# Turning x from its one copy: half-group moves inside SBUF, planned transfers and a second store queue

## The chip, the cores and the metric

The kernel runs on one core of one Trainium2 chip. What counts is the device time of one execution in microseconds (us), from the first to the last instruction and what lies around them. Five engines run side by side, each with its own queue of instructions that it works off in order: PE (matrix products), ACT (activations), DVE (vector work), POOL and SP (which here only issues transfers, or DMAs). They wait for one another by semaphores.

## The reference

An attention with learned inducing points is followed by a feed-forward layer with squared ReLU. x has 4 batches of 12480 tokens of 128 channels; there are 32 inducing points; the feed-forward layer is 2048 wide.

```python
def mab(q, kv):
    s = scale * (q @ kv.transpose(0, 2, 1))
    s = s - s.max(-1, keepdims=True)
    a = np.exp(s)
    a /= a.sum(-1, keepdims=True) + 1e-09
    return a @ kv
h = mab(I, x)            # 32 points attend to 12480 tokens, in each batch
y = mab(x, h)            # each token attends to the 32 results
...
h = np.maximum(y @ w_in, 0.0)
return (h * h @ w_out).astype(np.float32)
```

## The kernel before

**Tiles.** Tokens go in lanes of 480 (32 x 15). Four lanes make a group of 1920 tokens; a batch has six such groups and one of two lanes, so 26 lanes. A lane is also a block of the feed-forward layer: 104 blocks in all, and they make up most of the time. For the second product of a block, weights and activations are split into a high and a low part of the type fp32r (`hi`, `lo`, `wo_hi`, `wo_lo`), and three products of these stand for one in fp32 (L1027). The first two blocks are "plain": their second product is in fp32 (L984) and needs no split.

**Two attentions.** For each group of a batch, the first attention (class `First`, L396, for batches 1 to 3; `FirstBatch`, L550, for batch 0) needs x twice: as `xn` (rows of tokens, for the mixing product, L518 and L619) and transposed as `xt` (channels on the partitions, for the scores, L465 and L696). In batch 0 PE transposes (L671) and ACT or DVE copies (L254). In later batches `turn_blocks` (L429) loads x a second time: eight transfers for two lanes (L440) bring 32x32 blocks into `xb`, of which there is one buffer, and one DVE instruction turns them into `xt` (L443). `weigh` (L453) then takes scores, a running maximum, the exponential, a transpose of it (`et`) and the mix. In batch 0 the scores of groups 0 to 3 are kept in SBUF until one maximum of all seven groups is known (L569 to L585); then come seven exponentials, transposes and mixes (L603 to L619). `first_end` (L718) joins the sums (`htp`, L740), and multiplies the result by w_in once per batch (`wp`, L753, in four pieces, into `hw`, L757 and L762). `Second` (L780) takes each group's scores against the joined result (`na`, L796), its softmax on DVE and ACT, and copies the weights `sw` four times over the partitions into the tiles `st`, one for each lane (`spread`, L839, four transfers a lane, eight for the lanes of the two-lane groups, L843). A small copy of it (`mini`) serves only the first block of all. A block's first product `h` (L942) reads `hw` and `st`, so the feed-forward layer's first product and the second attention's last are one.

**A block.** `ffn_block` (L916) works in four quads: `h` (L942), relu and square on ACT (L949, L963), the cast `hi` and the rest `lo` on DVE (L968, L973), products into `op` (L1027, one in fp32 from the unsplit weights at L1017). DVE turns the result into `ob` (L1048), and four transfers on SP store it (L1054). The last block of all does that in two parts, of eight and seven rows.

**Who sets the order.** Each step is a task with an engine, a cost in ns, a due time, the tasks it needs and the buffers it takes (`Plan.add`, L68). `Plan.run` (L83) places them at build time: whenever an engine comes free, it takes the task that can start and is due first. So every engine's order is written out before the kernel runs, and an engine that has to wait for one instruction holds up all that stand behind it. The costs and due times are constants in the code. A load of eight blocks of x is booked at 2050 ns (L448), the spread of one lane at 800 (L908), the store of a block at 400 (L1061). x loads are due 20 us ahead of their use (L448). T_MAIN and BLOCK give the due times of the blocks, W_DUE those of the eight pieces of weights, S2_LEAD_0 and S2_LEAD the lead of the second attention, S1_LEAD that of the first. GATES (L193) lists weight tasks that the plan holds back until a step of the mini is done. Buffers are counted in the plan: XBB is the number of `xb`, XTB of `xt` (7, a batch's worth), XNB of `xn` (2), STB of `st` (6).

Of the kernel before, what the change touches and what calls it, by code (L numbers as in the profile page):

```python
# [20 lines left out]
P = 128  # L21
S = 32
# [140 lines left out]
def induced_attention_then_squared_relu_ffn(  # L163
# [232 lines left out]
    class First:  # L396
# [3 lines left out]
        def __init__(self, b, g, due, begun=None):  # L400
# [19 lines left out]
            for h in range(self.L // 2):  # L420
                self.turned.append(self.turn_blocks(h, due - 6000 + 3000 * h))
# [7 lines left out]
        def turn_blocks(self, h, due):  # L429
            b = self.b  # L430
            bb = Buffer("xb")
            v = {}

            def load():
                v["xb"] = xb_pool.tile([P, 2, NR, S], F32, tag="xb", name=f"xb_{self.n}_{h}")
                for l in range(2):
                    at = self.at + (2 * h + l) * LANE
                    rows = x[b, at:at + LANE, :].rearrange("(t r) (g c) -> g t r c", r=NR, c=S)
                    for c in range(P // S):
                        nc.sync.dma_start(v["xb"][c * S:(c + 1) * S, l], rows[c])  # L440

            def turn():
                nc.vector.transpose(  # L443
                    self.xt_tile()[:, 2 * h:2 * h + 2].rearrange("c l r t -> c (l r t)"),
                    v["xb"].rearrange("p l r c -> p (l r c)"),
                )
# [103 lines left out]
    class FirstBatch:  # L550


        def __init__(self, due, step, mix_due, mix_step):
            self.s = s = state.setdefault(0, {"xt": {}, "bxt": {}, "turned": {}})
            s["first"] = self
            self.sp, self.xn, self.bsp = {}, {}, {}
            self.loaded, self.tops, bxs = [], [], []
            v = {}
# [3 lines left out]
            kept = NG - 3  # L562

            for g in range(NG):
                self.group(g, due + step * g, g < kept, bare)

            def lanes():
                v["mx"] = tiny.tile([P, 1], F32, tag="mx", name="mx_0")
                nc.vector.tensor_reduce(v["mx"], bare[:, 0, :NG], axis=AX.X, op=ALU.max)  # L569

            def lanes2():
                v["lanes"] = tiny.tile([P, Q], F32, tag="lanes", name="lanes_0")
                nc.vector.tensor_scalar_mul(v["lanes"], lane_q, v["mx"])

            def gather():
                v["tops"] = self.last_sp[:, LANE:LANE + Q]
                nc.tensor.matmul(v["tops"], same, v["lanes"], start=True, stop=True)

            def most():
                v["top"] = tiny.tile([P, 1], F32, tag="top", name="top_0")  # L580
                nc.vector.tensor_reduce(v["top"], v["tops"], axis=AX.X, op=ALU.max)

            def shift():
                self.neg = tiny.tile([P, 1], F32, tag="neg", name="neg_0", bufs=4)
                nc.vector.tensor_scalar_mul(self.neg, v["top"], -scale)  # L585

            d = mix_due
            bg = self.bsp[NG - 1]
            t = add("DVE", 100, lanes, d - 3000, self.tops)
            t = add("DVE", 110, lanes2, d - 3000, [t])  # L590
            t = add("PE", 110, gather, d - 3000, [t], reads=[bg])
            t = add("DVE", 100, most, d - 3000, [t], reads=[bg])
            shifted = add("DVE", 70, shift, d - 3000, [t])
            bn = Buffer("s")
            powered, mixed = None, None
            for g in range(NG):
# [4 lines left out]
                def power(g=g, R=R, c=c):  # L601
# [3 lines left out]
                        bias=self.neg[:R], scale=scale, accum_out=bare[:R, 1, g:g + 1],  # L605
# [8 lines left out]
                def mix(g=g, R=R, c=c):  # L614
                    if g == 0:
                        v["nb"] = early_bank("nb_0")[:, :C]
                    for r in range(NR):
# [3 lines left out]
                            start=g == 0 and r < Q, stop=g == NG - 1 and r >= NR - Q,  # L621
                        )

                d = mix_due + mix_step * g
                powered = add("ACT", 820, power, d, [shifted, powered], takes=[be], reads=[self.bsp[g]])
                t = add("DVE", wide_ns(LANE), turn_e, d + 1000, [powered], takes=[bet], reads=[be])
                mixed = add("PE", 950, mix, d + 2000, [t, mixed], mode="n", takes=[] if g else [bn],
                            reads=[bet, self.bx[g]] + ([bn] if g else []))

            def add_h():  # L630
                self.acc = att.tile([P, C], F32, tag="hacc", name="hacc_0")
# [11 lines left out]
        def group(self, g, due, kept, bare):  # L643
# [4 lines left out]
            if g == 0:  # L648
                self.bxs = {}
# [493 lines left out]
```

## Time and profile before

| what | value |
|---|---|
| median of 3 | 1652.6 us (1652.34 to 1657.75) |
| the profiled execution | 1653.15 us |
| its span, first to last instruction | 1651.4 us |
| instructions | 22141 |
| bytes moved | 101.30 MB in 389085 packets, 368848 of them under 512 B |
| read from HBM, written to it | 48.94 MB, 25.56 MB |
| transfers `xb<-in_x_dram` | 312 of 60 KB, median 2.6 us from issue to landing |
| transfers `st<-sw` of 60 KB | 380, median 2.0 us |
| transfers `out_dram<-ob` of 60 KB | 412, median 2.2 us |

Times in the profile are microseconds from the span's start, unless marked ns. PEld is the loading of weights into PE, beside its products. "SPq" is SP's queue, which issues transfers. A row such as `PE h L942 <- DMA st<-sw` says that PE stood idle ahead of an instruction of line 942 that writes `h`, and that the landing of the transfer that fills `st` from `sw` ended the wait. In the chain of work that ended last, each piece stands with its start, its length and its name; it is followed back from the last instruction, at each step to what released it.

### The profile page before, as it was taken

The numbers are of one execution on the slowest core, as the hardware profiler recorded it, in microseconds if no ns is written. First come the engines' busy times: TensorE is split into PE (matmuls) and PEld (weight loads), VectorE is DVE, ScalarE is ACT, GpSimd is POOL, SyncE is SP. The second block draws the span as 40 slices with busy tenths as digits, with TensorE's granted clock in tenths as the row PEclk, the third lists the DMA queues.
The fourth block names the chain that finished last, engine by engine and source line by source line (L and its number), as shares of the span: only waits on it lengthen the run. The fifth ranks groups of instructions, "written<-read, shape, count | busy, mean of one in ns | idle before, by whom it ended". The sixth has DMA issues, their size and how long they took to land.

```text
span 1651.4 us, 22141 instructions
## 1 busy us (share of the span) xinstructions
PE 1615.4 (98%) x8004; PEld 1282.1 (78%) x8004; DVE 1535.6 (93%) x1457; ACT 1526.3 (92%) x1425; POOL 45.1 (3%) x39
## 2 busy tenths in 40 slices
PE   7889999999999999999999999999999999999998
PEld 5368787887778788888877778878787878888886
DVE  6759999999989999999999999999999999999997
ACT  5679999999989999999989999999999999999997
POOL 0000000000000000000000000000000000000000
PEclk9999999999999999999999999999999999999999
DMA  7441533422243333323233334233012212111211
GB/s 246 111 87 43 100 56 69 70 44 60 49 86 71 59 68 79 57 49 77 41 63 78 76 60 91 47 67 73 13 31 43 40 24 51 37 31 19 43 30 19
DMA packets 389085, 101.30 MB, mean 61 GB/s; under 512 B 368848, under 2 KB 385136, under 8 KB 388976
## 3 DMA queue, kind: packets, MB, share of 16 engines
q1 hardware_dynamic: 388976, 99.89, 29.8%
q8 instruction: 63, 1.03, 0.3%
q14 instruction: 46, 0.38, 0.1%
HBM read 48.94 MB, written 25.56 MB: 45 GB/s over the span
## 4 chain that ended last, share of the span: by engine, by line
PE 89%; DVE 5%; SPq 2%; issue 2%; DMA 1%; ACT 1%; DVEq 0%; POOL 0%; ACTq 0%
PE op L1027 57%; PE h L942 21%; PE op L1017 5%; DVE lo L973 2%; SPq L440 1%; PE nb L518 1%; PE na L796 1%; DVE hi L968 1%; PE sp L465 1%; PE op L984 1%; PE xtp L671 1%; SPq L843 1%; PE wp L753 1%; DVE hw L762 0%; DMA st<-sw 0%
## 5 line engine op out<-in xcount | busy, mean ns | idle before, releaser
L949 ACT ACTIVATE g<-h 128x960 f32<-128x960 f32 x832 | 780.4, 983 | 63.8 <-PE h L942 46.5
L973 DVE TENSOR_TENSOR lo<-g,hi 128x1920 fp32r<-128x1920 f32 (+1 forms) x409 | 823.7, 2015 | 15.2 <-DVE z L823 0.3
L963 ACT ACTIVATE g<-g 128x1920 f32<-128x1920 f32 (+1 forms) x419 | 760.2, 1814 | 4.5
L942 PE MATMUL h<-st,hw 128*128 128x480 f32 x1664 | 516.0, 392 | 6.4 <-DMA st<-sw 5.1
L968 DVE CAST hi<-g 128x1920 fp32r<-128x1920 f32 (+1 forms) x409 | 442.6, 1082 | 47.7 <-ACT g L963 39.7
L1027 PE MATMUL op<-hi,wo_hi 128*128 128x480 f32 x1530 | 442.5, 403 | 0.0
L1027 PE MATMUL op<-hi,wo_lo 128*128 128x480 f32 x1530 | 435.7, 383 | 0.0
L1027 PE MATMUL op<-lo,wo_hi 128*128 128x480 f32 x1530 | 415.4, 381 | 0.6 <-DVE lo L973 0.6
L942 PEld LDWEIGHTS h<-st,hw 128*128 128x128 f32 x1664 | 309.0, 188 | 93.9 <-issue 28.2
L1027 PEld LDWEIGHTS op<-hi,wo_hi 128*128 128x128 f32 x1530 | 286.2, 188 | 81.4 <-issue 36.6
L1027 PEld LDWEIGHTS op<-lo,wo_hi 128*128 128x128 f32 x1530 | 286.6, 188 | 54.8 <-issue 5.9
L1027 PEld LDWEIGHTS op<-hi,wo_lo 128*128 128x128 f32 x1530 | 287.2, 188 | 49.1 <-issue 3.0
L1017 PE MATMUL op<-g,wo_whole 128*128 128x480 f32 x204 | 98.9, 566 | 0.0
L820 POOL TENSOR_SCALAR z<-z 128x15 f32<-128x15 f32 (+1 forms) x28 | 44.0, 1571 | 1535.8 <-DVE z L816 1453.3
L1048 DVE STREAM_TRANSPOSE ob<-op 128x480 f32<-128x480 f32 (+1 forms) x105 | 70.3, 670 | 3.2 <-PE op L1027 2.9
L443 DVE STREAM_TRANSPOSE xt<-xb 128x960 f32<-128x960 f32 x39 | 45.2, 1159 | 14.3 <-DMA xb<-in_x_dram 11.3
L1017 PEld LDWEIGHTS op<-g,wo_whole 128*128 128x128 f32 x204 | 38.3, 189 | 7.5 <-issue 1.6
L518 PE MATMUL nb<-xn,et 128*32 128x128 f32 (+1 forms) x630 | 23.4, 282 | 5.7 <-DVE et L510 5.7
L518 PEld LDWEIGHTS nb<-xn,et 128*32 128x32 f32 (+1 forms) x630 | 17.5, 112 | 13.0 <-DVE et L510 6.5
L796 PE MATMUL na<-xt,hT 128*32 128x480 f32 (+1 forms) x224 | 26.9, 551 | 0.0
L465 PE MATMUL sp<-xt,indT 128*32 128x480 f32 x156 | 22.5, 578 | 2.2 <-DVE xt L443 2.2
L254 ACT CAST sw<-a 128x480 fp32r<-128x480 f32 (+1 forms) x25 | 14.2, 570 | 8.9 <-DVE a L830 8.8
(132 smaller groups left out, 469.7 us busy)
## 6 DMA issues: line engine op xcount, KB each, us to landing
out_dram<-ob SPq DMA_DIRECT2D x412, 60.0 KB, 2.2
xn<-in_x_dram SPq DMA_DIRECT2D x24, 960.0 KB, 5.1
st<-sw SPq DMA_DIRECT2D x380, 60.0 KB, 2.0
xb<-in_x_dram SPq DMA_DIRECT2D x312, 60.0 KB, 2.6
xn<-in_x_dram SPq DMA_DIRECT2D x4, 480.0 KB, 5.1
hi_i<-in_moe_w_in_dram SPq DMA_DIRECT2D x2, 512.0 KB, 14.5
lo_i<-in_moe_w_in_dram SPq DMA_DIRECT2D x2, 512.0 KB, 17.4
hi_o<-in_moe_w_out_dram SPq DMA_DIRECT2D x2, 512.0 KB, 4.3
```

The lines of the kernel that those rows point to most:

```text
L443: nc.vector.transpose(self.xt_tile()[:, 2 * h:2 * h + 2].rearrange("c l r t -> c (l r t)"), v["xb"].rearrange("p l r c -> p (l r c)"),)
L518: nc.tensor.matmul(v["nb"][c * M:(c + 1) * M, :], self.et[:R, r, :], self.xn[:R, r, :], start=r < Q, stop=r >= NR - Q,)
L796: nc.tensor.matmul(v["na"][i * M:(i + 1) * M, :W], s["hT"][:, :M], cols[:, c:c + W], start=True, stop=True,)
L820: E.tensor_scalar(v["z"], v["z"], 1e-9, 0.0, ALU.add, ALU.add)
L942: nc.tensor.matmul(c["hp"][:, l, :LANE], s["hw"][:, f * P:(f + 1) * P], second.st[k], start=True, stop=True,)
L949: nc.scalar.activation(v["g"][:, 2 * i:2 * i + 2, :], c["hp"][:, :, :LANE], AF.Relu)
L963: nc.scalar.activation(v["g"][:, h], v["g"][:, h], AF.Square)
L968: nc.vector.tensor_copy(v["hi"][:, h], v["g"][:, h])
L973: nc.vector.tensor_sub(v["lo"][:, h], v["g"][:, h], v["hi"][:, h])
L1017: nc.tensor.matmul(w["op"][:, :LANE], wo_whole, v["g"][:, 3, :], start=False, stop=False)
L1027: nc.tensor.matmul(w["op"][:, :LANE], pools["wo"][wo][:, 4 * j + l, :], v[name][:, l, :], start=(j == x_ == 0 and l == 0), stop=(j == NQ - ...
L1048: nc.vector.transpose(w["ob"][:, rows].rearrange("p r c -> p (r c)"), w["op"][:, rows.start * S:rows.stop * S])
```

## The change

It has five parts.

1. In batches 1 to 3, x is no longer loaded a second time. Each group is turned in two halves, of 64 channels each, straight from `xn` into one of two buffers `xb` (XBB is 2), by one DVE instruction; then transfers inside SBUF move each block of 32 channels of each lane to its place in `xt`: eight for half a group of four lanes, four for half a group of two. So the transfers' number (16 or 8 a group) stays, and the groups of two lanes need two turns where they needed one. The turn waits for `xn`; the move waits for the turn and takes the `xt` buffer.
2. Transfers are booked in the plan with other costs: 1240 ns for each lane of a move, 2480 for each piece of a spread, 2600 for a store. Moves have the due time of their turn.
3. Batch 0's first attention runs in two parts, groups 0 to 4 and groups 5 and 6, each with a maximum of its own; the first part's sums are faded when they are added to the second's. Five groups' scores are kept, not four, and an exponential waits for its own group's kept scores.
4. The last block's second store goes out by ACT's queue, not SP's.
5. Constants: due times, leads and steps have other values; the pieces 1 to 3 of batch 0's `wp` go into the banks `m`, not `h`, and they and the first copy of `hw` are held back by other steps of the mini; the mini's `sk` takes a buffer of `xb`.

```diff
-    GB, HB, LB, OB, MB, STB, XTB, XNB, XBB = 3, 2, 2, 2, 2, 6, 7, 2, 1
-    T_MAIN, BLOCK = 42100.0, 15100.0
+    GB, HB, LB, OB, MB, STB, XTB, XNB, XBB = 3, 2, 2, 2, 2, 6, 7, 2, 2
+    T_MAIN, BLOCK = 48600.0, 15100.0
-    W_DUE = [11900.0, 21100.0, 24900.0, 30200.0, 41500.0, 46000.0, 50000.0, 53300.0]
-    FIRST_DUE, FIRST_STEP, MIX_DUE, MIX_STEP, MINI_DUE = 6000.0, 2600.0, 25000.0, -1000.0, -800.0
-    S2_LEAD, S2_LEAD_0, S2_STEP, S1_LEAD, S1_STEP = 44500.0, 26000.0, 1600.0, 11100.0, 3000.0
+    W_DUE = [20500.0, 27300.0, 31000.0, 32500.0, 43500.0, 42700.0, 47000.0, 53600.0]
+    FIRST_DUE, FIRST_STEP, MIX_DUE, MIX_STEP, MINI_DUE = 5800.0, 3100.0, 22400.0, 200.0, -1000.0
+    S2_LEAD, S2_LEAD_0, S2_STEP, S1_LEAD, S1_STEP = 40500.0, 30000.0, 1400.0, 10900.0, 3600.0
...
-        s0=m.ready[0], s1=m.ready[0], s2=m.ready[0], s3=m.ready[0], w0_1=m.normed, w0_2=m.normed, w0_3=m.normed,
+        s0=m.ready[0], s1=m.ready[0], s2=m.ready[0], s3=m.ready[0], w0_1=m.ready[0], w0_2=m.ready[0], w0_3=m.ready[0], p0_0=m.powered,
...
-    SPLIT_DUE, SPLIT_STEP, PLAIN_DUE = 64000.0, 0.0, 9500.0
+    KEPT = 5
+    SPLIT_DUE, SPLIT_STEP, PLAIN_DUE = 65000.0, 200.0, 6000.0
-    G1_DUE, SQ_DUE, HI_DUE, LO_DUE, OP_DUE = -1500.0, 6000.0, 2500.0, 6500.0, 10300.0
-    OT_DUE = 7900.0
+    G1_DUE, SQ_DUE, HI_DUE, LO_DUE, OP_DUE = -2500.0, 6200.0, 4500.0, 6500.0, 14100.0
+    OT_DUE = 6100.0
...
-            for h in range(self.L // 2):
-                self.turned.append(self.turn_blocks(h, due - 6000 + 3000 * h))
+            for h in range(2):
+                self.turned.append(self.turn_blocks(h, due - 8000 + 4000 * h))
             self.weigh(due + 2000, S1_STEP)
...
         def turn_blocks(self, h, due):
-            def load():
-                v["xb"] = xb_pool.tile([P, 2, NR, S], F32, tag="xb", name=f"xb_{self.n}_{h}")
-                for l in range(2):
-                    at = self.at + (2 * h + l) * LANE
-                    rows = x[b, at:at + LANE, :].rearrange("(t r) (g c) -> g t r c", r=NR, c=S)
-                    for c in range(P // S):
-                        nc.sync.dma_start(v["xb"][c * S:(c + 1) * S, l], rows[c])
-
             def turn():
+                v["xb"] = xb_pool.tile([P, 2, NR, S], F32, tag="xb", name=f"xb_{self.n}_{h}")
                 nc.vector.transpose(
-                    self.xt_tile()[:, 2 * h:2 * h + 2].rearrange("c l r t -> c (l r t)"),
-                    v["xb"].rearrange("p l r c -> p (l r c)"),
+                    v["xb"][:R].rearrange("p j r t -> p r j t"),
+                    self.xn[:R, :, 2 * h * S:2 * (h + 1) * S].rearrange("p r (j c) -> p r j c", j=2),
                 )
-            t = state["blocks"] = add("SP", 2050, load, due - 20000, [state.get("blocks"), self.begun], takes=[bb], late=0)
-            t = state["turn"] = add("DVE", 1090, turn, due, [t, state.get("turn"), self.begun],
-                                    takes=[] if h else [self.bt], reads=[bb] + ([self.bt] if h else []))
-            return t
+            def move():
+                xt = self.xt_tile()
+                for j in range(2):
+                    c0 = (2 * h + j) * S
+                    for q in range(self.L):
+                        nc.sync.dma_start(xt[c0:c0 + S, q], v["xb"][q * M:(q + 1) * M, j])
+
+            t = state["turn"] = add("DVE", 1090, turn, due, [self.loaded, state.get("turn"), self.begun],
+                                    takes=[bb], reads=[self.bx])
+            return add("SP", 1240 * self.L, move, due, [t] + self.turned, late=0, takes=[] if h else [self.bt],
+                       reads=[bb] + ([self.bt] if h else []))
...
+            self.kept = kept = KEPT
+            for i, span in enumerate([range(kept), range(kept, NG)]):
+                prev = self.part(i, span, prev, bare, [mix_due - kept * mix_step, mix_due][i], mix_step)
...
+            def fade():
+                v["fade"] = tiny.tile([P, 1], F32, tag="fade", name="fade_0")
+                nc.scalar.activation(v["fade"], prev["neg"], AF.Exp, bias=new["neg"], scale=-1.0)
...
+                    nc.vector.scalar_tensor_tensor(new["acc"], prev["acc"], v["fade"], v["nb"], ALU.mult, ALU.add)
...
-            if b:
+            if b or k:
                 v["wp", k] = bank(f"wp_{b}_{k}")
...
-                t = self.ready[k] = state["spread"] = add("SP", 800, lambda k=k: spread(k), d + 8 * step,
+                t = self.ready[k] = state["spread"] = add("SP", 2480 * len(to[k]), lambda k=k: spread(k), d + 8 * step,
...
         def store(rows):
+            queue = nc.scalar if last_block and rows.start else nc.sync
             for c in range(P // S):
-                nc.sync.dma_start(out_v[c][:, rows], w["ob"][c * S:(c + 1) * S, rows])
+                queue.dma_start(out_v[c][:, rows], w["ob"][c * S:(c + 1) * S, rows])
...
-            add("SP", 400, lambda rows=rows: store(rows), end + 6000, [t])
+            add("ACT" if last_block and rows.start else "SP", 2600, lambda rows=rows: store(rows), end + 6000, [t])
```

More of the change, by code (lines that the diff above doesn't have):

```diff
@@ L561, in __init__, with part, most_of @@
             nc.gpsimd.memset(bare[:, 1], 0.0)
-            kept = NG - 3
+            self.kept = kept = KEPT
             for g in range(NG):
-                self.group(g, due + step * g, g < kept, bare)
+                self.group(g, due + step * g, bare)
+            prev = None
+            for i, span in enumerate([range(kept), range(kept, NG)]):
+                prev = self.part(i, span, prev, bare, [mix_due - kept * mix_step, mix_due][i], mix_step)
+        def part(self, i, span, prev, bare, due, step):
+            v, new = {}, {}
+            last = span[-1]
+            def most_of():
+                v["mx"] = tiny.tile([P, 1], F32, tag="mx", name=f"mx_0_{i}")
+                nc.vector.tensor_reduce(v["mx"], bare[:, 0, span.start:span.stop], axis=AX.X, op=ALU.max)
@@ L567, in lanes @@
             def lanes():
[L568 to L572, printed above, removed]
+                v["lanes"] = tiny.tile([P, Q], F32, tag="lanes", name=f"lanes_0_{i}")
                 nc.vector.tensor_scalar_mul(v["lanes"], lane_q, v["mx"])
             def gather():
-                v["tops"] = self.last_sp[:, LANE:LANE + Q]
+                v["tops"] = self.bank[last][:, LANE:LANE + Q]
@@ L587, in __init__ @@
[L587 to L593, printed above, removed]
+                new["neg"] = tiny.tile([P, 1], F32, tag="neg", name=f"neg_0_{i}", bufs=4)
+                if prev:
+                    nc.vector.scalar_tensor_tensor(new["neg"], v["top"], -scale, prev["neg"], ALU.mult, ALU.min)
+                else:
+                    nc.vector.tensor_scalar_mul(new["neg"], v["top"], -scale)
@@ new lines, in fade @@
+            def fade():
+                v["fade"] = tiny.tile([P, 1], F32, tag="fade", name="fade_0")
+                nc.scalar.activation(v["fade"], prev["neg"], AF.Exp, bias=new["neg"], scale=-1.0)
+            bg = self.bs[last]
+            t = add("DVE", 100, most_of, due - 3000, [self.tops[g] for g in span])
+            t = add("DVE", 110, lanes, due - 3000, [t])
+            t = add("PE", 110, gather, due - 3000, [t], reads=[bg])
+            t = add("DVE", 100, most, due - 3000, [t], reads=[bg])
@@ L594, in __init__ @@
+            shifted = new["shifted"] = add("DVE", 70, shift, due - 3000, [t, prev and prev["shifted"]])
             bn = Buffer("s")
-            powered, mixed = None, None
-            for g in range(NG):
+            powered, mixed = prev and prev["powered"], prev and prev["mixed"]
+            for g in span:
                 R = M * lanes_of[g]
@@ L620, in mix @@
                             v["nb"][k * M:(k + 1) * M, :], c["et"][:R, r, :], self.xn[g][:R, r, :],
-                            start=g == 0 and r < Q, stop=g == NG - 1 and r >= NR - Q,
+                            start=g == span[0] and r < Q, stop=g == last and r >= NR - Q,
                         )
-                d = mix_due + mix_step * g
-                powered = add("ACT", 820, power, d, [shifted, powered], takes=[be], reads=[self.bsp[g]])
+                d = due + step * (g - span[0])
@@ L630, in add_h @@
+            new["powered"], new["mixed"] = powered, mixed
             def add_h():
[L631 to L639 removed]
@@ L641, in induced_attention_then_squared_relu_ffn @@
-        bx = property(lambda self: self.bxs)
-        def group(self, g, due, kept, bare):
+                new["acc"] = att.tile([P, C], F32, tag="hacc", name=f"hacc_0_{i}")
+                if prev:
+                    nc.vector.scalar_tensor_tensor(new["acc"], prev["acc"], v["fade"], v["nb"], ALU.mult, ALU.add)
+                else:
+                    copy(new["summed"], new["acc"], v["nb"])
+                self.acc = new["acc"]
+            def add_z():
+                new["z"] = tiny.tile([P, 1], F32, tag="z", name=f"z_0_{i}")
+                nc.vector.tensor_reduce(new["z"], bare[:, 1, span.start:span.stop], axis=AX.X, op=ALU.add)
+                self.sum = new["z"]
+                if prev:
+                    self.sum = tiny.tile([P, 1], F32, tag="zs", name="zs_0")
+                    nc.vector.scalar_tensor_tensor(self.sum, prev["z"], v["fade"], new["z"], ALU.mult, ALU.add)
@@ L644, in group @@
+            f = add("ACT", 250, fade, due, [shifted]) if prev else None
+            d = due + step * len(span)
+            self.totalled = new["totalled"] = add("DVE", 250 if prev else 100, add_z, d, [powered, f, prev and prev["totalled"]])
+            self.summed = new["summed"] = add("DVE", 260, add_h, d + 1000, [mixed, f, prev and prev["summed"]], reads=[bn])
+            return new
+        def group(self, g, due, bare):
             s = self.s
@@ L708, in group @@
             t = add("PE", 950, score, due + 1200, turned_, mode="n", takes=[bs], reads=[bt])
[L709 to L710 removed]
+            self.tops[g] = add("DVE", wide_ns(LANE), top, due + 2000, [t], reads=[bs])
+            if g < self.kept:
                 self.bsp[g] = Buffer("st")
```

55 lines of the change are left out of this document (23 added, 32 removed).

## The prediction

> **What bounds the kernel now.** I read the page's busy times first, then a table by stage, then who waited for whom, then the chain of work that ended last and the transfer queue in the stages that the table marks.
>
> ```profile
> PE 1615.4 (98%) x8004; PEld 1282.1 (78%) x8004; DVE 1535.6 (93%) x1457; ACT 1526.3 (92%) x1425; POOL 45.1 (3%) x39
> ```
>
> PE is busy almost throughout, so the average tells little: what a change can win lies where PE stands still. The table by stage shows where that is (us of the stage, then busy us of PE, weight loads, DVE, ACT, POOL, the granted clock, the share of the DMA engines, GB/s).
>
> ```profile
> core 0 of [0], span 1651.4 us
> core 0: us, PE busy (x) PEld busy (x) DVE busy (x) ACT busy (x) POOL busy (x), PEclk, DMA share, GB/s
> 20.00:45.00 25.00, 18.26 (x283) 12.62 (x281) 23.05 (x51) 14.31 (x28) 0.00 (x0) 0.86 0.60 191
> 45.00:54.00 9.00, 7.50 (x29) 2.67 (x29) 6.43 (x19) 2.97 (x6) 0.00 (x0) 0.81 0.68 165
> 54.00:72.00 18.00, 14.39 (x49) 6.19 (x50) 14.82 (x27) 16.18 (x18) 1.01 (x1) 1.00 0.23 41
> 72.00:90.00 18.00, 12.25 (x59) 7.08 (x56) 9.39 (x20) 9.01 (x11) 0.29 (x1) 0.81 0.38 68
> 90.00:108.00 18.00, 18.00 (x56) 10.19 (x55) 6.52 (x7) 15.68 (x14) 0.00 (x0) 1.00 0.62 136
> 420.00:470.00 50.00, 47.23 (x237) 34.85 (x236) 45.26 (x51) 42.45 (x43) 0.32 (x1) 0.99 0.29 60
> 470.00:830.00 360.00, 360.00 (x1785) 290.51 (x1785) 347.66 (x319) 343.51 (x317) 12.00 (x7) 1.00 0.33 64
> 830.00:880.00 50.00, 47.65 (x266) 35.30 (x265) 46.80 (x53) 41.69 (x43) 0.32 (x1) 1.00 0.35 72
> 1630.00:1651.40 21.40, 14.85 (x65) 11.81 (x63) 13.37 (x13) 9.75 (x9) 0.00 (x0) 0.96 0.16 23
> ```
>
> From 470 to 830 PE never rests, and neither removed loads nor a quieter HBM can shorten that stretch. There are four places left: the start, where DVE is the full engine (23.05 of 25 us); the first blocks, 54 to 90 us, where PE lacks 9.4 us (3.61 and 5.75); the two changes of batch, where it lacks 2.8 and 2.4; and the end. PE's waits after the start name the causes (waiter, releaser: us in total, times, longest).
>
> ```profile
> PE nb L518 <- DVE et L510: 5.7, 1, 5.7
> PE h L942 <- DMA st<-sw: 5.1, 2, 2.8
> PE sp L465 <- DVE xt L443: 2.2, 1, 2.2
> ```
>
> The first and third lie in the first blocks; there the transfer queue and the chain read:
>
> ```profile
> 63.03 5.24 SPq L440 DMA_DIRECT2D xb<-in_x_dram  x8
> 68.38 7.54 SPq L843 DMA_DIRECT2D st<-sw  x12
> 76.02 6.23 SPq L440 DMA_DIRECT2D xb<-in_x_dram  x8
> ```
>
> ```profile
> 81.62 2.79 DMA xb<-in_x_dram
> ...
> 84.72 1.18 DVE xt L443
> 85.90 0.53 DVE z L816
> 86.44 0.60 DVE et L510
> 87.08 1.93 PE nb L518 x30
> ```
>
> SP needs about 0.65 us for each of these issues, so eight are 5.2 to 6.2 us, where the plan booked 2050 ns, and four spreads are 2.5 us, where it booked 800. DVE stood behind a load that the plan believed landed, and PE behind DVE. The second wait, for st, is at the changes of batch:
>
> ```profile
> 458.19 5.27 SPq L440 DMA_DIRECT2D xb<-in_x_dram  x8
> 463.56 2.48 SPq L843 DMA_DIRECT2D st<-sw  x4
> ```
>
> ```profile
> 465.46 1.95 DMA st<-sw
> ```
>
> Eight loads for a group that is scored tens of us later (they go by a due time 20 us ahead of their use) stand in front of the four copies that the next block cannot start without.
>
> **The start (L553 and on).** Now all seven groups of batch 0 share one maximum; after the change groups 0 to 4 have their own, and 5 and 6 follow with a fade. The chain shows:
>
> ```profile
> 23.25 0.94 PE sp L696 x8
> ...
> 31.72 0.14 DVE neg L585
> ...
> 44.24 0.47 PE htp L740 x2
> ```
>
> ```profile
> 53.97 0.48 PE L942 MATMUL h<-st,hw 128*128 128x480 f32 x1
> ```
>
> The last row, of PE's timeline, is the first h of the first block. By my count of the score rows, the one at 23.25 is the fifth group. From the shift at 31.72 to the join at 44.24 are 12.5 us for seven groups, 1.8 each, with weight decoding between them on DVE. If only two groups were left behind the last maximum, that would be 3.6 us, a gain of 8.9 at the most. Against it stands DVE at 23.05 of 25 us: the decoding only changes places (W_DUE), and what is put off is due again soon after. Added are a second chain of maximum, shift and sums, some seven tiny instructions at the 0.14 us of the shift's row, 1.0 us, and one more copy of scores (KEPT is 5, not 4), perhaps half a microsecond. Bounds: 8.9 gained to 1.5 lost. I take half of the gain less the additions: **4 gained**. The moved banks and gates of the first products (wide, GATES) work in the same chain and are in that figure; the mini's sk now takes an xb buffer, which is free before the first turn, so it costs nothing unless that turn is early.
>
> **The first blocks.** Per full group, 16 loads of x go and 16 moves inside SBUF come: the number of issues on SP is the same, and by the rows above their price is too (5.24/8 = 0.65 for a load, 7.54/12 = 0.63 for a copy of the moves' shape). So SP is not relieved. What changes is what DVE waits for: its turn now reads xn, which one big load brought, and no longer a burst of eight issues. The 5.7 us wait cannot come in this form. And the plan now books 4960 ns for eight moves, 2480 for four spreads, 2600 for a store. But a move is a new wait in SP's queue: it waits for the turn, for its half-group buffer and for an xt buffer that the last batch's scores must release; behind it on SP stand spreads, for which PE's h waits, and stores, for whose ob buffers DVE's L1048 and then the op bank wait. The moves' due times are ahead of those of the first twelve spreads, so a burst may still stand in front of them. At stake are the 9.4 us of idle PE, and the clock: 72 to 90 shows 0.81 on 12.25 busy us, at most 2.3 lost. Bounds: 11.7 gained to 0. I leave two waits of the size of the 2.2 us row, 4.4 in all: **7 gained**. The Trainium skill (TensorE: Matmul & The Clock Gate, Part 1) says that an idle PE falls to half its clock and needs some 3.4 us of work to get it back. The row 0.81 agrees that the gate closed here; by that rule the sum would be a microsecond or so better if the long wait goes, since its wake goes too.
>
> **The changes of batch.** No load of a far group can slip in front of st any more, since a move needs a turned half-group and a free xt buffer; and the second attention starts from an earlier due time (S2_LEAD_0 30 us, not 26). Bounds: the 5.1 us that PE waited for st, to 0 if moves of the next batch's first group take the loads' place: they are due 18.9 and 14.9 us ahead of the block (10.9 + 8, and 4 later), the spread 18.8 (30 less 8 steps of 1.4). I take **4 gained**.
>
> **The end.** The last eight stores:
>
> ```profile
> 1645.37 3.80 SPq L1054 DMA_DIRECT2D out_dram<-ob  x8
> DMA to landing us min/median/max: 1.6/1.6/1.7
> ```
>
> 3.80/8 is 0.475 us an issue. With the second four on ACT they no longer stand behind the first four: 1.9 us saved if ACT issues as fast, which no row shows; 0 if it is twice as slow. I take **1.7 gained**. The Trainium skill (DMA: Bandwidth & Descriptors, Issuing engines are not separate DMA queues) speaks against this edit: both queues feed the same engines, and only issue time is saved, "which is usually small relative to the DMA itself". By that the term would be near 0 and the sum 1.7 us worse. Here 1.9 us of issue stand beside 1.6 to land, so it isn't small.
>
> **The steady stretch.** DVE turns 42 half-groups in place of 39 (the groups of two lanes now need two). A half-group is still 960 elements a partition, but read and written in runs of 32.
>
> ```profile
> L443 DVE STREAM_TRANSPOSE xt<-xb x39: 1117/1167/1205, 61.8 to 1191.1; 128x960 f32<-128x960 f32 x39
> L254 DVE COPY xt<-xtp x3: 1090/1092/1225, 9.5 to 21.3; 128x896 f32<-128x896 f32 x2, 128x1024 f32<-128x1024 f32 x1
> ```
>
> The second row writes xt in runs of 32 and takes 1.22 ns an element, the first 1.22 without them; so runs seem to cost nothing. The three more turns are 3.5 us of DVE; from 470 to 830 it has 12.3 of 360 to spare. Bounds 0 to 3.5 lost, **1 lost** taken. Cover gone, each turn's delay would be PE's.
>
> **The sum.** -4 - 7 - 4 - 1.7 + 1 = -15.7. The profiled execution took 1653.15 us around its span of 1651.4; the median is 1652.6, 0.55 below it. Predicted: 1652.6 - 15.7 = 1636.9, so 1637. About 0.5% (8.3 us) is what a measurement of this kernel tells from no change.
>
> **Rivals.** *More is won*: two groups only behind the last maximum, all of the waits gone: -8.9 - 11.7 - 5.1 - 1.9 = -27.6, 1625. For it: those waits come from wrong bookings, which are mended. Against: DVE's full start. Chance 0.13.
>
> *The queue keeps its bursts*: as many issues at the same price, moves ahead of spreads as the loads were. Only start, end and the three turns count: -4 - 1.7 + 1 = -4.7, 1648. For it: equal issue counts and the due times above. Against: the bookings now match the rows. Chance 0.16.
>
> *Slower, the score waits for the moves*: until now x was prefetched to the turn, and PE waited for a turn once in 21 groups. Now behind each turn come 8 issues and 2 us to land before PE may score, and SP, in order, often sits at the head of its queue:
>
> ```profile
> SPq L1054 <- DVE ob L1048: 398.5, 54, 25.9
> ```
>
> A move that stands behind such a store is late, and PE, in order too, stands at the score with all blocks' products behind it. Priced by the longest wait for st, 2.8 us: at all 21 groups 58.8, at 11 of them 30.8 - 15.7 = +15, 1668. It outweighs the gain from 6 groups on (15.7/2.8), and makes it slower by over 0.5% from 9. Against it: moves are due 10 and 6 us ahead of the score, and PE's order comes from a plan that now books them fully. Chance 0.11.
>
> **How the numbers follow.** Forecast 0.60, own range 1627 to 1642 (the start and the first blocks both at their best, or both at half). With 0.13 at 1625 and 0.16 at 1648 around it, 1620 to 1656 leaves out the third rival and some tails, 0.2. Faster 0.60 + 0.13 = 0.73, same 0.16, slower 0.11.
>
> **What would show it.** Right: the first h near 50; no wait of DVE's turn for a transfer; PE idle in the first 36 us of blocks below 5 us; no wait of h for st at the changes of batch; two queues at the end, with the last landing 1.7 us after less issuing. Wrong: PE waits at sp for moves, a median turn above 1.3 us, or gaps in the stretch that is full now.

## The result and the profile after

| | before | after |
|---|---|---|
| median of 4 runs each | 1653.25 us (1652.34 to 1657.75) | 1643.59 us (1642.27 to 1643.93) |
| ratio after/before, 95% interval | | 0.9935 (0.9915 to 0.9954) |
| the profiled execution's span | 1651.4 us | 1641.5 us |

By the medians the kernel became 9.7 us faster, 0.58%; by the ratio, 0.65%, and its interval leaves no change out. That is 6 us short of the 15.7 us that the sum gave: 1643.59 us lies inside the wide range of 1620 to 1656, but 1.6 us above the forecast's own range, 1627 to 1642. The page of the kernel after has these lines of busy times, packets, bytes from HBM, the turn (busy us, mean ns of one, then the idle time of DVE ahead of it) and the moves (median us to landing):

```profile
PE 1615.2 (98%) x8006; PEld 1277.3 (78%) x8006; DVE 1538.8 (94%) x1476; ACT 1525.8 (93%) x1418; POOL 48.8 (3%) x39
...
DMA packets 249308, 101.29 MB, mean 62 GB/s; under 512 B 219088, under 2 KB 245360, under 8 KB 249200
...
HBM read 29.77 MB, written 25.56 MB: 34 GB/s over the span
...
L437 DVE STREAM_TRANSPOSE xb<-xn 128x960 f32<-128x960 f32 (+1 forms) x42 | 48.9, 1164 | 15.0 <-DMA out_dram<-ob 6.3
...
xt<-xb SPq DMA_DIRECT2D x312, 60.0 KB, 2.0
```

The change does what it says: 19 MB less are read from HBM, packets fall by a third, there are 42 turns of 1164 ns and as many moves as there were loads. The column to look at is the last of the turn's row: DVE stood idle for 15.0 us ahead of turns, for transfers. The table by stage of the kernel after (columns as in the prediction: PE, weight loads, DVE, ACT, POOL, granted clock, DMA share, GB/s):

```profile
20.00:45.00 25.00, 20.41 (x301) 11.44 (x300) 23.04 (x63) 14.26 (x29) 0.00 (x0) 0.93 0.43 132
45.00:54.00 9.00, 5.33 (x12) 3.37 (x13) 8.53 (x21) 4.15 (x6) 0.00 (x0) 0.66 0.70 275
54.00:72.00 18.00, 17.23 (x58) 7.49 (x56) 16.99 (x29) 15.52 (x19) 0.89 (x1) 0.98 0.31 73
72.00:90.00 18.00, 17.90 (x82) 9.98 (x81) 6.51 (x15) 16.68 (x17) 0.29 (x1) 1.00 0.41 88
90.00:108.00 18.00, 14.48 (x61) 9.68 (x59) 9.27 (x7) 16.27 (x14) 0.00 (x0) 1.00 0.50 127
420.00:470.00 50.00, 50.00 (x278) 37.45 (x277) 47.83 (x53) 46.17 (x47) 0.32 (x1) 1.00 0.42 100
470.00:830.00 360.00, 359.38 (x1786) 289.00 (x1785) 347.83 (x324) 342.90 (x315) 11.99 (x7) 1.00 0.29 62
830.00:880.00 50.00, 49.91 (x250) 37.10 (x249) 48.42 (x50) 45.04 (x44) 1.23 (x2) 1.00 0.37 85
```

From 54 to 90 us PE's idle time fell from 9.4 to 0.9 us, and the clock of 72 to 90 from 0.81 is full. At the two changes of batch it fell from 5.1 to 0.1. But from 90 to 108, where PE was full, it now lacks 3.5 us. PE's waits from 54 us to the end of the kernel after (waiter, releaser: us in total, times, longest) name that one, and no wait for `st` or at `sp` is left:

```profile
PE op L1049 <- DVE hi L990: 4.4, 2, 3.8
PE h L964 <- ACT g L971: 0.7, 2, 0.4
```

It is one chain over three engines. SP's queue, then DVE's and PE's timeline of the kernel after (start, length, what; in brackets the idle time ahead and its releaser):

```profile
84.03 10.60 SPq L863 DMA_DIRECT2D st<-sw  x16
94.67 5.02 SPq L447 DMA_DIRECT2D xt<-xb  x8
99.74 0.58 SPq L412 DMA_DIRECT2D xn<-in_x_dram  x1
```

```profile
97.54 2.16 DVE L995 TENSOR_TENSOR lo<-g,hi 128x1920 fp32r<-128x1920 f32 x1
105.96 1.18 DVE L437 STREAM_TRANSPOSE xb<-xn 128x960 f32<-128x960 f32 x1 [6.26 <-DMA out_dram<-ob]
107.06 1.12 DVE L990 CAST hi<-g 128x1920 fp32r<-128x1920 f32 x1
```

```profile
103.35 1.13 PE L964 MATMUL h<-st,hw 128*128 128x480 f32 x4
108.24 1.15 PE L1049 MATMUL op<-hi,wo_hi 128*128 128x480 f32 x4 [3.76 <-DVE hi L990]
```

Sixteen spreads and eight moves occupied SP for 15.6 us; only then was the big load of the next group's `xn` issued, although its buffer had been free since about 78 us (the mix that last read it ran from 77.1 to 78.0). The load takes some 5 us to land. The turn reads `xn`, so it waited 6.3 us. The row's releaser is a store, but the turn doesn't touch what a store reads; e6 below shows that it was the load. Behind the turn, in order, stood the cast `hi`, and behind that PE's products. The wait has an aftermath in the clock. The same table for the 12 us around it:

```profile
104.00:108.00 4.00, 0.48 (x3) 0.08 (x1) 2.04 (x2) 3.33 (x3) 0.00 (x0) 1.00 0.47 91
108.00:112.00 4.00, 3.76 (x14) 2.59 (x18) 4.00 (x4) 0.60 (x1) 0.00 (x0) 0.67 0.00 0
112.00:116.00 4.00, 4.00 (x20) 2.19 (x13) 4.00 (x7) 3.52 (x4) 0.00 (x0) 0.91 0.19 47
```

A clock of 0.67 and then 0.91 over 4 us each loses 1.3 + 0.4 = 1.7 us more, so the wait of 3.76 us cost about 5.5. The Trainium skill (TensorE: Matmul & The Clock Gate, Part 1) has the clock fall to half after an idle window of some 3.4 us, and come back after as long a busy one; the trace agrees, since 1.7 us lost at half speed are 3.4 us of it.

### The profile page after: what moved, and what is told of

Its sections match the earlier page's. It is cut to its first block, busy times and chain, and to the rows that moved or that the text cites. A ratio compares the mean times of both kernels' runs of the same rounds, so it can differ in the third digit from the quotient of the medians.

```text
span 1641.5 us, 22177 instructions
## 1 busy us (share of the span) xinstructions
PE 1615.2 (98%) x8006; PEld 1277.3 (78%) x8006; DVE 1538.8 (94%) x1476; ACT 1525.8 (93%) x1418; POOL 48.8 (3%) x39
## 4 chain that ended last, share of the span: by engine, by line
PE 92%; DVE 3%; SPq 2%; ACT 1%; DMA 1%; issue 1%; DVEq 0%; ACTq 0%
PE op L1049 60%; PE h L964 22%; PE op L1039 5%; PE na L816 1%; PE nb L519 1%; PE sp L466 1%; DVE lo L995 1%; SPq L863 1%; PE wp L773 1%; SPq L447 1%; ACT g L971 0%; PE op L1006 0%; DVE hi L990 0%; PE xtp L691 0%; DMA xn<-in_x_dram 0%
## 5 line engine op out<-in xcount | busy, mean ns | idle before, releaser
L964 PE MATMUL h<-st,hw 128*128 128x480 f32 x1664 | 529.1, 400 | 2.4 <-DVE st L898 1.5
L1049 PE MATMUL op<-hi,wo_hi 128*128 128x480 f32 x1530 | 434.5, 394 | 4.4 <-DVE hi L990 4.4
L1049 PE MATMUL op<-hi,wo_lo 128*128 128x480 f32 x1530 | 428.8, 381 | 0.0
L1049 PE MATMUL op<-lo,wo_hi 128*128 128x480 f32 x1530 | 424.3, 382 | 0.6 <-DVE lo L995 0.4
L840 POOL TENSOR_SCALAR z<-z 128x15 f32<-128x15 f32 (+1 forms) x28 | 47.7, 1703 | 1522.2 <-DVE z L836 1509.2
L437 DVE STREAM_TRANSPOSE xb<-xn 128x960 f32<-128x960 f32 (+1 forms) x42 | 48.9, 1164 | 15.0 <-DMA out_dram<-ob 6.3
L832 ACT ACTIVATE d<-d 128x480 f32<-128x480 f32 (+1 forms) x28 | 16.2, 579 | 5.9 <-DVE d L829 5.8
```

Source lines behind the costliest of these rows:

```text
L437: nc.vector.transpose(v["xb"][:R].rearrange("p j r t -> p r j t"), self.xn[:R, :, 2 * h * S:2 * (h + 1) * S].rearrange("p r (j c) -> p r j ...
L840: E.tensor_scalar(v["z"], v["z"], 1e-9, 0.0, ALU.add, ALU.add)
L964: nc.tensor.matmul(c["hp"][:, l, :LANE], s["hw"][:, f * P:(f + 1) * P], second.st[k], start=True, stop=True,)
L1049: nc.tensor.matmul(w["op"][:, :LANE], pools["wo"][wo][:, 4 * j + l, :], v[name][:, l, :], start=(j == x_ == 0 and l == 0), stop=(j == NQ - ...
```

## The experiments

My theory after the result: the gain came from the bookings alone (part 2 of the change), since the plan now knows how long SP is held; and x from its one copy (part 1) costs time, since DVE's turn, and what stands behind it in order, hangs on SP's queue twice, for a late `xn` and for a free `xb`. The rival is the one that the change's looks suggest: it gained by reading 19 MB less, and the bookings only rearranged the waits. The start and the end were tested for their own terms. Each run has its own median of the kernel before, on the same chip, beside it; gains are best compared by the ratios.

**e1, the end alone.** The kernel before, with the last store's second part on ACT's queue.

```diff
+            queue = nc.scalar if last_block and rows.start else nc.sync
             for c in range(P // S):
-                nc.sync.dma_start(out_v[c][:, rows], w["ob"][c * S:(c + 1) * S, rows])
+                queue.dma_start(out_v[c][:, rows], w["ob"][c * S:(c + 1) * S, rows])
```

> The kernel before with one edit: the second of the last two stores goes out by ACT's queue. If issue time on SP was what the end waited for (theory A), the last landing comes about 1.6 us earlier and the time is 1651.6 against 1653.2. If both queues share what limits the end, nothing changes: 1653.2.

1652.78 us against 1654.02 (ten and nineteen runs), ratio 0.9987 (0.9978 to 0.9997): 1.2 us by the medians, 2.1 by the ratio. In its profile 5.05 us pass from the end of the last product to the end of the span, where it was 6.55 before. In the kernel after, the two queues' last issues are these:

```profile
1637.35 1.95 ACTq L1077 DMA_DIRECT2D out_dram<-ob  x4
```

```profile
1637.05 1.86 SPq L1077 DMA_DIRECT2D out_dram<-ob  x4
```

ACT issues at 0.49 us apiece, SP at 0.47: side by side they need 2.3 us where the prediction's row showed 3.8.

**e2, the start in one part.** The kernel after, with one maximum for all seven groups.

```diff
-            for i, span in enumerate([range(kept), range(kept, NG)]):
+            for i, span in enumerate([range(NG)]):
```

> The changed kernel with batch 0's first attention in one part again (one maximum for all seven groups), all else as changed. Theory A (the start is full of DVE work that only changes places): within 1.5 us of the changed kernel, 1642 to 1645. Theory C (the two parts are worth the 4 us that were forecast): 1647 to 1648, with the first h later and what PE loses up to 90 us greater by 4.

1645.31 against 1654.02, ratio 0.9941 (0.9925 to 0.9956). The first h stands at 57.7 us, 8.4 later than in the kernel after (49.3), and the time is 1.7 us longer by the medians, 1.0 by the ratios, whose intervals overlap: just above theory A's range by the medians, and short of theory C's. The due times here were set for two parts; the kernel before, with its own, has its first h at 53.97. So against this run a first block that starts 8.4 us earlier brings 1 to 2 us at the end. The chain of the kernel after shows part of the reason:

```profile
39.63 0.47 PE htp L760 x2
...
43.55 4.25 DMA lo_o<-in_moe_w_out_dram
...
48.46 0.51 ACT st L894
...
49.30 1.97 PE h L964 x4
```

The join is 4.6 us earlier than before, as is the first h (49.30, not 53.97). But from 45 to 54 us DVE is busy for 8.53 of 9 us and PE for only 5.33, at a clock of 0.66: the decoding that was put off is due there. The last product of block 0 ends at 65.0 us, where it ended at 66.7 before, and block 1's first `op` starts at 67.1, not 67.5: little of the 4.7 us is left. And e2 has no wait at 104 us (PE is busy for all 18 us from 90 to 108), so it is no clean price of the two parts: the kernel after has the earlier start and that wait. e6 below has two parts without the wait, and stands 4.3 us below e2 by the ratios, with intervals that just overlap.

**e3, the same bytes from HBM.** The kernel after, but each move is replaced, at its place in the queue, by a transfer of 60 KB from HBM.

```diff
-                        nc.sync.dma_start(xt[c0:c0 + S, q], v["xb"][q * M:(q + 1) * M, j])
+                        at = self.at + q * LANE
+                        rows = x[self.b, at:at + LANE, :].rearrange("(t r) (g c) -> g t r c", r=NR, c=S)
+                        nc.sync.dma_start(xt[c0:c0 + S, q], rows[2 * h + j])
```

> The changed kernel, in which each move inside SBUF is replaced by a load of the same 60 KB from HBM in runs of 128 bytes into the same place, at the same point of the same queue (so xt holds x in the wrong layout, and a move no longer waits for the turn). Theory A (the order of the transfers is what counted, not their kind): 1641 to 1645. Theory B (the gain is the 19 MB of small packets that left HBM): back towards the kernel before, 1648 to 1653.

1638.82 against 1654.02, the middle of three executions (a fourth, of 3215.88 us, is left out), ratio 0.9909 (0.988 to 0.9938). With the 19 MB back on HBM the kernel is not slower than the kernel after. The traffic saved is worth nothing that shows here, and the rival falls; in the kernel after, the DMA engines are busy for a share of 0.29 in the long stretch. Why e3 is rather faster it can't say by itself, since its transfers also don't wait for the turn.

**e4, the old bookings.** The kernel after, with 2050 ns for eight moves, 800 for each spread, 400 for a store.

```diff
-            return add("SP", 1240 * self.L, move, ...
+            return add("SP", 2050 * self.L // 4, move, ...
-                t = self.ready[k] = state["spread"] = add("SP", 2480 * len(to[k]), ...
+                t = self.ready[k] = state["spread"] = add("SP", 800, ...
-            add("ACT" if last_block and rows.start else "SP", 2600, ...
+            add("ACT" if last_block and rows.start else "SP", 400, ...
```

> The changed kernel with the old bookings of transfers in the plan (2050 ns for eight moves, 800 for each spread, 400 for a store). Theory A (right bookings order the queue): the burst waits of the first blocks and of the changes of batch come back, 1649 to 1655. Theory B (traffic) and a gain by the moves alone: 1642 to 1645.

1653.92 against 1654.02, ratio 0.9998 (0.9988 to 1.0008). Nothing is left of the gain, with the other four parts of the change in place. DVE's waits, and PE's at the changes of batch in the table by stage:

```profile
DVE xb L437 <- DMA xt<-xb: 21.2, 10, 3.7
DVE xb L437 <- DMA out_dram<-ob: 9.1, 1, 9.1
```

```profile
420.00:470.00 50.00, 47.56 (x261) 35.19 (x260) 44.31 (x52) 41.70 (x41) 0.32 (x1) 0.97 0.38 85
470.00:830.00 360.00, 357.16 (x1746) 284.64 (x1748) 344.88 (x317) 339.41 (x312) 14.55 (x7) 1.00 0.28 61
830.00:880.00 50.00, 47.44 (x257) 34.81 (x257) 44.69 (x50) 40.02 (x39) 0.32 (x1) 0.97 0.40 103
```

PE lacks 2.4 and 2.6 us at the changes of batch again, and 2.8 in the stretch between them. DVE waits 21 us for an `xb` that moves, up to sixteen issues in a row on SP, have not yet emptied.

**e5, the bookings alone.** The kernel before, with three constants changed.

```diff
-            t = state["blocks"] = add("SP", 2050, load, ...
+            t = state["blocks"] = add("SP", 5200, load, ...
-                t = self.ready[k] = state["spread"] = add("SP", 800, ...
+                t = self.ready[k] = state["spread"] = add("SP", 2480 * len(to[k]), ...
-            add("SP", 400, lambda rows=rows: store(rows), end + 6000, [t])
+            add("SP", 2600, lambda rows=rows: store(rows), end + 6000, [t])
```

> The kernel before with one edit: the plan books transfers at what they take on SP (5200 ns for the eight loads of x, 2480 for a spread, 2600 for a store). x is still loaded twice. If right bookings are the whole gain (theory A1): 1643 to 1647. If they need the moves, since loads that are due 20 us ahead of their use still stand in front of spreads (theory A2): 1650 to 1655, with PE's wait for st at the changes of batch still there.

1636.57 against 1653.58, ratio 0.9898 (0.9879 to 0.9918): 17 us, 7 more than the whole change, and better than either theory had asked for. SP's queue at the first change of batch, and the table by stage:

```profile
449.87 10.07 SPq L843 DMA_DIRECT2D st<-sw  x16
460.04 3.56 SPq L1054 DMA_DIRECT2D out_dram<-ob  x4
463.65 5.52 SPq L440 DMA_DIRECT2D xb<-in_x_dram  x8
```

```profile
54.00:72.00 18.00, 16.58 (x55) 7.97 (x53) 16.89 (x32) 16.92 (x20) 0.89 (x1) 1.00 0.18 33
72.00:90.00 18.00, 16.00 (x52) 7.82 (x54) 8.83 (x16) 15.21 (x17) 0.29 (x1) 0.91 0.46 92
...
420.00:470.00 50.00, 50.00 (x278) 37.53 (x278) 48.46 (x54) 44.73 (x45) 0.32 (x1) 1.00 0.35 72
470.00:830.00 360.00, 360.00 (x1793) 289.74 (x1792) 348.26 (x322) 343.76 (x317) 11.98 (x7) 1.00 0.33 65
830.00:880.00 50.00, 50.00 (x250) 38.88 (x250) 49.17 (x52) 44.99 (x43) 1.56 (x2) 1.00 0.42 81
```

The four last spreads that stood behind a burst of loads at 463.56 now stand ahead of it, though the loads were not touched. Both changes of batch are full, and the long stretch between them has no gap. From 54 to 90 us PE lacks 3.4 us, where it lacked 9.4, and the clock of 72 to 90 is 0.91, not 0.81.

**e6, one load earlier.** The kernel after, with the `xn` load of 99.74 us put ahead of the sixteen spreads, by moving it in the list that the plan returns.

```diff
+    order.remove(loads[2])
+    order.insert(order.index(spreads[3]), loads[2])
```

> The changed kernel with one transfer moved in SP's written order: the third big load of x of the later batches, which stood behind 16 spreads and 8 moves for 21 us after its buffer was free, goes in front of them. Theory A (the turn's new wait for this load cost what the first blocks gave back): DVE's 6.3 us wait and PE's wait at 104 us go, 4 us less, 1639 to 1640. Rival (that wait lay beside waits of ACT, which is full there): at most 1 us less, 1642.5 to 1644.

1638.82 against 1653.58, ratio 0.9915 (0.9898 to 0.9932): 4.8 us better than the kernel after by the medians, 3.3 by the ratios. SP's queue and DVE's timeline:

```profile
84.59 0.55 SPq L412 DMA_DIRECT2D xn<-in_x_dram  x1
85.66 10.67 SPq L863 DMA_DIRECT2D st<-sw  x16
```

```profile
98.30 2.16 DVE L995 TENSOR_TENSOR lo<-g,hi 128x1920 fp32r<-128x1920 f32 x1
100.38 1.17 DVE L437 STREAM_TRANSPOSE xb<-xn 128x960 f32<-128x960 f32 x1
```

The turn follows without a gap. PE is busy for all 18 us of 90 to 108, and the clock stays full to 126. So the wait was for that load, and most of the 5.5 us that idle time and clock add up to came back.

**e7 and e8, the start's late weights, and all loads early.** In e7 (the kernel after), ACT's first step of the last piece of w_out, which waits for the transfer of 4.25 us in the chain above, goes behind the first copy of `st`. e8 adds to it that each `xn` load goes out as soon as the plan has its buffer free, which moves two loads.

```diff
+    order.remove(size)
+    order.insert(order.index(kept) + 1, size)
```

> The changed kernel with one instruction moved in ACT's written order: the first step of the last piece of w_out, which waited 4.25 us for its load in front of the copy that fills the first st, goes behind it. So the first h comes some 4 us earlier. Theory A (the start is full of DVE work that only changes places): the time stays within 1 us, 1642.5 to 1644.5. Theory C (an earlier first h is time won): 4 us less, 1639 to 1640.

> The changed kernel with the instruction of ACT moved as in the run before it, and with every big load of x put into SP's order as soon as the plan has its buffer free. Theory A: the turn's waits for loads go where the buffer was free earlier, 4 to 5 us less, 1638.5 to 1640. Theory C: 8 us less, 1635 to 1636. Neither helps: 1642.5 to 1644.

e7: 1643.47 against 1653.58, ratio 0.9943 (0.9924 to 0.9961), no change from the kernel after. The first h came no earlier (50.1 us): with ACT's wait gone, `st` waited for the mini's `sk`, whose steps on DVE stand among decoding steps. So e7 didn't tell what an earlier first h would be worth; it shows what was next late. e8: 1638.52, ratio 0.9914 (0.9897 to 0.9931), first h at 48.9: the same as e6 within the intervals.

**e9, bookings and end.** e5 with the edit of e1 (the store by ACT booked there).

> The kernel before with right bookings and with the last store on two queues, nothing else of the change. If the two parts add up: 17 us and 1.6 us less than before, 1634 to 1636, faster than the kernel before and the changed one.

1634.78 against 1653.59, ratio 0.9891 (0.9874 to 0.9909): 1.2 us by the ratios and 1.8 by the medians below e5, about what e1 gave by itself, though the intervals overlap.

**e10, the change without its one copy.** The kernel after, with the loads, the turn and the due time of the kernel before, eight loads booked at 5200; `xb` keeps its two buffers.

```diff
-            for h in range(2):
-                self.turned.append(self.turn_blocks(h, due - 8000 + 4000 * h))
+            for h in range(self.L // 2):
+                self.turned.append(self.turn_blocks(h, due - 6000 + 3000 * h))
...
+            t = state["blocks"] = add("SP", 5200, load, due - 20000, [state.get("blocks"), self.begun], takes=[bb], late=0)
+            t = state["turn"] = add("DVE", 1090, turn, due, [t, state.get("turn"), self.begun],
```

> The changed kernel with x loaded twice again: the turn reads eight-load half groups as before, booked at 5200 ns and due 20 us ahead; all else as changed. Theory M (the moves cost: the turn waits for the big load, and for buffers that moves free): 1633 to 1638, and what PE loses from 90 to 126 and from 880 to 1225 goes back to the size of the kernel before. Theory K (the other constants of the change cost): it stays at 1641 to 1645.

1633.49 against 1653.59, ratio 0.9878 (0.9862 to 0.9895): the lowest of all, though its interval overlaps with those of e5, e9 and e12, and 10.1 us better than the kernel after by the medians, 9.4 by the ratios. From 880 to 1225 us PE is busy for all 345 again. The table by stage, and DVE's only wait for a transfer ahead of a turn:

```profile
72.00:90.00 18.00, 18.00 (x81) 10.08 (x80) 7.09 (x11) 16.83 (x17) 0.29 (x1) 1.00 0.52 86
90.00:108.00 18.00, 18.00 (x80) 13.05 (x79) 14.82 (x14) 16.60 (x15) 0.00 (x0) 1.00 0.58 131
470.00:830.00 360.00, 360.00 (x1788) 288.47 (x1787) 348.40 (x325) 343.75 (x318) 12.47 (x7) 1.00 0.32 62
```

```profile
DVE xt L444 <- DMA xb<-in_x_dram: 5.5, 2, 4.2
```

**e11, bookings and moves.** The kernel before with parts 1 and 2 (`xb` twice, `sk` in a buffer of it), all other constants as before.

```diff
-    GB, HB, LB, OB, MB, STB, XTB, XNB, XBB = 3, 2, 2, 2, 2, 6, 7, 2, 1
+    GB, HB, LB, OB, MB, STB, XTB, XNB, XBB = 3, 2, 2, 2, 2, 6, 7, 2, 2
...
+            t = state["turn"] = add("DVE", 1090, turn, due, [self.loaded, state.get("turn"), self.begun],
+                                    takes=[bb], reads=[self.bx])
+            return add("SP", 1240 * self.L, move, due, [t] + self.turned, late=0, takes=[] if h else [self.bt],
```

> The kernel before with right bookings and with the moves of the change (two half-group buffers, the mini's sk in one of them), all other constants as before. Theory M: 4 to 8 us slower than right bookings alone, 1640 to 1645, with waits of DVE's turn for xn. Theory K: as fast as right bookings alone, 1635 to 1638.

1647.58 against 1653.59, ratio 0.9965 (0.9955 to 0.9975): 11 us slower than e5. The cost of the moves is the same from the other side, and more than I had expected. DVE's waits ahead of the turn:

```profile
DVE xb L436 <- DMA xt<-xb: 5.0, 3, 3.0
...
DVE xb L436 <- issue: 1.7, 1, 1.7
...
DVE xb L436 <- DMA xn<-in_x_dram: 1.4, 2, 0.8
```

**e12, bookings a little off.** e5 with 5500, 2600 and 2750, 5% more. It asks whether e5 was a lucky order, since every constant moves the whole plan.

> The kernel before with bookings 5 per cent above the right ones (5500, 2600, 2750 ns). If the gain of right bookings is that of their size: within 3 us of it, 1634 to 1640. If it was one lucky order of the plan: anywhere up to 1653.

1634.49 against 1653.59, ratio 0.9884 (0.9867 to 0.99). The gain stands with another order. In one table, with what DVE waited ahead of turns for transfers from 54 us on (the sum of the waits' rows):

| kernel | ratio | DVE's waits ahead of turns, us |
|---|---|---|
| before | 1 | 14.1 |
| after | 0.9935 | 15.0 |
| e4, old bookings in after | 0.9998 | 32.5 |
| e6, one load earlier in after | 0.9915 | 9.7 |
| e11, bookings and moves | 0.9965 | 6.4 |
| e5, bookings alone | 0.9898 | 0.8 |
| e10, after with loads | 0.9878 | 5.5 |
| e12, bookings 5% over | 0.9884 | none |

Among kernels with the right bookings, those whose turn reads the loads wait less and are faster, but the rank isn't strict: these waits are not the whole price of the moves.

## Why the prediction was right, and where it was not

The sum was right in sign, and the prediction right in that PE's waits came from wrong bookings. Two of its terms were mis-sized, one of its steps failed, and a loss as large as the net gain had no term of its own. By PE's idle time in the tables by stage:

- **The start: 4 forecast, 0 found.** From 20 to 54 us PE lacks 8.2 us before and 8.3 after. The first h is earlier by 4.7 us, but the decoding put off fills DVE behind it. "What is put off is due again soon after" was in the working; half of the bound was still too much. How much two parts are worth by themselves stays open: 1 to 1.7 us by e2, which lacks the wait at 104 us, 4.3 by the ratios of e2 and e6, where neither has it. Between kernels that each have their own constants it is little: e10, with two parts, stands 2.1 us below e9, with one (0.9878 and 0.9891), and the intervals overlap.
- **The first blocks: 7 forecast, 5.0 found** (idle from 54 to 108: 9.4 before, 0.9 + 3.5 after). The waits of before did go, by more than was left for them. The clock, which isn't in these 5.0, gave 2.3 us back from 72 to 90 (0.81 on 12.25 busy us) and took 1.7 from 108 to 116. The step that failed is "the 5.7 us wait cannot come in this form". The turn reads what one big load brought, true; but that load stands in the same queue, behind the same bursts, with only two buffers `xn`. "No wait of DVE's turn for a transfer" was wrong: 15.0 us of them after, 14.1 before.
- **The changes of batch: 4 forecast, 5.0 found.** The reason was half right. I gave it to the moves (a move needs a turned half); e5 shows that with the loads left in place the bookings alone put the spreads first, and e4 that moves with the old bookings don't.
- **The end: 1.7 forecast, 1.6 found**: from the last product's end to the end of the span 6.55 us (1644.85 to 1651.4) and 5.0 (1636.5 to 1641.5). The Trainium skill's sentence that issue time "is usually small relative to the DMA itself" (DMA: Bandwidth & Descriptors, Issuing engines are not separate DMA queues) doesn't hold for these stores: four issues take 1.86 us, a landing 1.7.
- **The steady stretch: 1 lost forecast, 1.9 found**, all other stages taken together. The turn itself costs what was said: its median is 1170 ns with runs of 32, 1167 before. PE's gaps there are 0.6 us from 470 to 830 and 1.2 from 880 to 1225, where it had none before (345.00 busy) and has none in e10; DVE waits in these two stretches for late `xn` loads (4.3 us) and full `xb` (2.4). Gaps in the stretch that was full were one of the signs of being wrong that the prediction named. The longer stretch after the change:

```profile
880.00:1225.00 345.00, 343.78 (x1714) 275.55 (x1712) 331.51 (x306) 329.18 (x304) 12.41 (x7) 1.00 0.27 57
```

Added up: 0 - 5.0 - 5.0 - 1.6 + 1.9 = -9.7, and the span fell by 9.9.

Of the rivals, *more is won* failed at the start and at the new wait. *The queue keeps its bursts* is refuted by e4 and e5: with as many issues at the same price, their bookings alone are worth 17 us. *Slower, the score waits for the moves* named the right part and the wrong place. PE never waits at `sp`, since the moves are due early enough; the turn ahead of them is what waits, and DVE's casts behind it. Its price is about 10 us, too little to turn the sign, because the bookings bring 17. The working priced the parts by the stages in which they act, and so gave neither the bookings nor the moves a term of their own: +17 and -10 lay hidden in stages that were each about right. That the total came out as near as it did is in part luck. The bookings aren't quite all of the gain either: e11, with bookings and moves alone, stands at 0.9965 and the kernel after at 0.9935, so the other three parts bring some 5 us there; with loads in place of moves, e5 at 0.9898 and e10 at 0.9878, some 3.

Open is where all of the 10 us goes. From e10 to the kernel after, PE's idle time grows by some 4 us from the span's start to the last product (3.5 of it from 90 to 108), and the clock's loss at 108 to 116 is 1.7. e6, which removes that one wait and its loss, still stands at 0.9915 where e10 has 0.9878, 6 us apart. About half of the 6 shows in the profiles: from 126 to 1225 us PE idles for 3.1 us in e6 and for 0.4 in e10. Another 3 us or so are clock in the start (0.86 on 21.34 busy us from 20 to 45 in e6, 1.00 in e10), and no run tells whether the moves have a part in it. PE's recorded busy time is 1615.2 us in the kernel after and 1608.9 in e10 for as many products. Of these 6.3 us, 1.7 are the clock at 108 to 116 and 1.4 that of 20 to 45 (0.93 on 20.41 busy us, against 1.00); since the ends of products are modelled, the profile doesn't say in which of them the rest lies. That three `xn` buffers would mend it wasn't tried.

## What to carry to other kernels

Where a plan writes out each engine's order, the time that a queue's issues really hold it is part of the kernel: three constants, set to what the trace shows, gave 17 us, more than a rebuilt data path beside them. A transfer that an in-order engine waits for is only as early as the queue it stands in; ask for each new wait what its source waits for, one step further back. And price each part of a change by itself against the kernel without it, since a part that costs 10 us can ride unseen on one that brings 17.

The version to keep is e10, the change without its one copy of x: 1633.49 us, 0.9878 (0.9862 to 0.9895). The kernel before with three bookings 5% over (e12, 0.9884) can't be told from it.

## What the runs showed of the hardware

- What an issue holds SP for doesn't go by its bytes in these runs: 0.63 us for a move of 60 KB inside SBUF (5.02 us for eight), 0.66 for a spread of 60 KB (10.60 for sixteen), but 0.33 to 0.58 for a load of `xn`, most of which are 960 KB, with a median of 0.45. The last stores of 32 KB take 0.47 (1.86 for four). Landing takes a median of 2.0 us for the moves, and 2.6 for the same bytes from HBM in e3.
- A DVE transpose of 128x960 costs the same whether it reads and writes in runs of 32 or not: 1170 and 1167 ns.
- A single PE gap of 3.76 us was followed by 1.7 us lost in the clock.
- Bytes from HBM were no limit at a DMA share of 0.3: with 19 MB more of them the kernel after was not slower (e3, 0.9909, and e10, 0.9878, against 0.9935).
